# Polysketch attention with an ELU feed-forward: the key work of later batches in later steps, batch 1's key features through ScalarE, and one GpSimd rounding instead of four

## The chip, the cores and the metric

The kernel runs on one core of a Trainium2 chip. A core has five engines that run side by side, each with its own queue of instructions: TensorE (PE) for matrix products and its weight loads (PEld), VectorE (DVE), ScalarE (ACT), GpSimd (POOL) and SyncE (SP), which here only issues transfers. An engine takes its instructions in the order of the program and waits on semaphores for what other engines produce. The metric is the time of one execution on the device, in microseconds (us); lower is better.

## The reference

```
q, k, v: (4 batches, 4 heads, 1088 positions, 32) float32;  S1, S2: (8, 32)
phi(x)  = outer(S1 x, S2 x), flattened to 64 features per position
kv = sum over s of phi(k) v^T        (64 x 32 per batch and head)
z  = sum over s of phi(k)            (64 per batch and head)
x  = (phi(q) kv) / (phi(q) z + 1e-6)           -> (4352, 128) after the heads are joined
h  = x @ w_in                        (128 -> 2048)
g  = h if h > 0 else exp(h) - 1      (ELU)
out = g @ w_out                      (2048 -> 128)
```

S1, S2, w_in and w_out arrive as 64-bit floats. The kernel turns them into float32 itself ("rounding" below), by integer operations on the two halves of each number.

## The kernel before

**Tiling.** The 4352 rows are cut into 68 half tiles of 64 and these into 9 groups g of up to 512 rows (the last has 256). The hidden size 2048 is cut into 8 chunk pairs cp of 256. One **step** is one (g, cp). `mm1` makes h for both chunks of the pair (L661), `elu` is two ScalarE operations (L677, L679) and one VectorE operation (L685) per chunk, and `mm2` adds the pair into the output bank `o0` or `o1` (L698). In step n TensorE does `mm1` of step n and `mm2` of step n - 2; there are 72 steps, and groups 0 and 1 take turns in the first sixteen. The buffers of h are four, so `mm1` of step n can begin only when `elu` of step n - 2 is done. `fin1` transposes a finished group and issues its output transfers on SP.

**Rounding.** Eleven roundings i turn weights into float32 as they arrive: 0 to 5 are 256 columns wide, 6 to 10 are 512 wide (w_in and w_out of one chunk pair; rounding 6 serves pair 3, and so on to rounding 10 for pair 7). `RA(i)` is one VectorE mask (L99), `RB(i)` one ScalarE operation (L104), `RC(i)` three VectorE operations (L112, L113, L117) and a last one, `round_e`, which is either one VectorE operation (L125) or, with `pool`, two on GpSimd (L122, L123).

**Attention.** For each batch b the keys go through `transp` (VectorE transpose, L235), `KF_late` (key features, TensorE, L312) with `KF_late_out` (VectorE transposes, L322), `KO_late` (two outer products, VectorE, L282), `KA_late` (the sums kv and z, TensorE, L340 and L344) with `KC_late` (ScalarE copies), and `KZ_late` with `KZ_late_out` and `KZ3` (TensorE, VectorE, GpSimd), which leave kvp and SWp for the queries. Batch 0 has its own functions ahead of the steps (`KF`, `KF_out`, `KO`, `KA`, ...; L298 and L397 are its key features and sums). Queries: `transp` of q, then `queries(g5, g1)` on TensorE, which holds the last product of group g5 (`q5`, L627) and the first of group g1 (`q1`, L492); `q1_out` (VectorE, L502), `q2` (VectorE, features) and `q4` (VectorE transpose, L617) lie between the two products of a group. `x0_eps` opens the sums of group 0 with four products that put 1e-6 into them (L554), `q1_first` is group 0's first product (L530). `keep_warm` multiplies ones into an unused bank (L221).

**Order.** The program is a list written by hand. Work ahead of the steps stands in plain order; in the steps, `at(n, f, ...)` puts a call between `mm1` and `elu` of step n, and `late(n, f, ...)` puts it after `elu` and ahead of `mm2`. The order within each engine's queue is that of these calls. Small PSUM tiles share the tag `aux` with two banks. Transfers are issued on SP in one list; the key and query tiles of a batch have two buffers each, so a load waits for the transpose that frees its buffer.

Of the kernel before, what the change touches and what calls it, by code (L numbers as in the profile page):

```python
# [12 lines left out]
F32 = mybir.dt.float32  # L13
# [9 lines left out]
def _ap(ap: bass.AP, free):  # L23
    return dataclasses.replace(ap, ap=[list(ap.ap[0])] + [list(x) for x in free])
# [3 lines left out]
def kernel(  # L28
# [20 lines left out]
    nc = tc.nc  # L49
    B, H, S, D = q.shape  # L50
    R = S1.shape[0]
    P = 128
# [4 lines left out]
    NT = S // 64  # L57
    KT = (NT + 1) // 2
# [5 lines left out]
    work = ctx.enter_context(tc.tile_pool(name="wk", bufs=2))  # L64
    psum = ctx.enter_context(tc.tile_pool(name="psum", bufs=2, space=bass.MemoryType.PSUM))
# [6 lines left out]
    kT = [const.tile([FD, 2 * KT, 64], F32, name=f"kT{b}") for b in range(B)]  # L72
    qT = [const.tile([FD, NT, 64], F32, name=f"qT{b}") for b in range(B)]
# [145 lines left out]
    def keep_warm(n, cols=256):  # L219
        for i in range(n):  # L220
            nc.tensor.matmul(idle[:, :cols], some[:, :P], some[:, :cols], skip_group_check=True)  # L221
# [12 lines left out]
    def transp(dst, x, b, t0, t1):  # L234
        nc.vector.transpose(dst[b][:, t0:t1, :].rearrange("p t (a c) -> p c t a", c=2), hd[x, b][:, :, t0:t1, :])  # L235
# [11 lines left out]
    Sab = const.tile([FD, H, 2 * R], F32, name="Sab")  # L247
    SW = const.tile([FD, H, 3, R], F32, name="SW")
    SWp = const.tile([FD, B, 2, 4, R], F32, name="SWp")
    keep_warm(3)  # L250
    keep_warm(1, 160)
    sps = psum.tile([P, 512], F32, name="sps", tag="aux")
    nc.tensor.matmul(sps[:, :2 * R], Sx[:].rearrange("p h d -> p (h d)"), ident[:2 * R, :2 * R])
    make_SX()
# [10 lines left out]
    def make_SXh():  # L265
        nc.gpsimd.tensor_add(Sxp[:].rearrange("p x c r -> p c x r"), Sab[:, :2].rearrange("p c (x r) -> p c x r", x=2),
                             Sab[:, 2:].rearrange("p c (x r) -> p c x r", x=2))
        nc.gpsimd.tensor_add(pmask[:], bmask[:, :2], bmask[:, 2:])
        nc.vector.tensor_reduce(hmask[:], _ap(zmask[:], [[1, H], [H, 4]]), axis=AX, op=ADD)
        nc.gpsimd.tensor_mul(SXh[:].rearrange("p (h d) -> p h d", h=H), SX[:].rearrange("p (h d) -> p h d", h=H),  # L270
                             _ap(hmask[:], [[1, H], [0, D]]))

    def make_SWp():
        nc.gpsimd.memset(SWp[:, :, :, 3, :], 0.0)
        for b in range(B):
            nc.gpsimd.tensor_add(SWp[:, b, :, :2, :].rearrange("p c x r -> p c (x r)"), Sab[:, :2], Sab[:, 2:])


    def outer(dst, ab):

        a_, b_ = ab[:, :, 1, :], ab[:, :, 0, :]
        nc.vector.tensor_mul(dst, _ap(a_, list(a_.ap[1:]) + [[0, R]]), _ap(b_, [b_.ap[1], [0, R], b_.ap[2]]))  # L282
# [6 lines left out]
    kv_ps, feats, zms, wzs, abps = {}, {}, {}, {}, {}  # L289
# [11 lines left out]
        abps[b] = [where[i] for i in (0, 4, 8)]  # L301

    def KF_late(b):
# [25 lines left out]

    def KA_late(b):

        kv = kv_ps[b] = psum.tile([P, 512], F32, name="kvl", **(dict(tag="aux") if b == 1 else dict(tag="o1", bufs=1)))
        ab = feats.pop(b)
        kp = [feats.pop((b, half)) for half in range(2)]
        for i in range(KT):
            for h in range(H):
                nc.tensor.matmul(kv[32 * h:32 * h + 32, :R * R], vt[b][:, (h * KT + i) * D:(h * KT + i + 1) * D],  # L340
                                 kp[i // 5][:, i % 5, h].rearrange("p i j -> p (i j)"),
                                 start=(i == 0), stop=(i == KT - 1), skip_group_check=True, tile_position=(0, 32 * h))
            c = 32 * (i % 4)
            nc.tensor.matmul(kv[c:c + 32, R * R:R * R + H * R], ab[:, 0, i].rearrange("p h r -> p (h r)"),  # L344
                             ab[:, 1, i].rearrange("p h r -> p (h r)"),
                             start=False, stop=(i >= KT - 4), skip_group_check=True, tile_position=(0, c))
# [29 lines left out]
    def KO(b, gi):  # L376
        ab, rows = feats[b, gi]
        n = len(KG[gi])
        kp = work.tile([P, 4, H, R, R], F32, name="kp", tag="kp", bufs=3)
        outer(kp[:rows, :n].rearrange("p t h i j -> p (t h) i j"),  # L380
              ab[:rows, :n].rearrange("p t h x r -> p (t h) x r"))
        feats[b, gi] = kp, rows
# [43 lines left out]
    def KZ3(b):  # L426
        z = wzs.pop(b)
        nc.gpsimd.tensor_add(SWp[:, b, :, 2, :], z[:, :2], z[:, 2:])
# [6 lines left out]
    def KS(b):  # L435
        nc.gpsimd.memset(kvp[:, b], 0.0)
        for hp in range(2):
            for f in range(2):
                for e in range(2):
                    r = 64 * e + 32 * hp  # L440
                    nc.gpsimd.tensor_copy(kvp[r:r + 32, b, f, :, hp, :],
                                          kvz[b][64 * hp + 32 * f:64 * hp + 32 * f + 32, :, hp, :D])
# [10 lines left out]
    def half_tile(g, k):  # L453
        return divmod(8 * g + k, NT)
# [70 lines left out]
    def q1_first():  # L525
        p = psum.tile([P, 512], F32, name="abqp", tag="aux")
        for i in range(4):
            for u in range(2):
                b, t = half_tile(0, 2 * i + u)
                nc.tensor.matmul(p[64 * u:64 * u + 64, i * 64:i * 64 + 64], qT[b][:, t, :],  # L530
                                 Sab[:].rearrange("p h y -> p (h y)"),
                                 skip_group_check=True, tile_position=(0, 64 * u))
        x = work.tile([P, 4 * H, 2, R], F32, name="abq", tag="abq", bufs=1)
        nc.scalar.copy(x[:].rearrange("p m x r -> p (m x r)"), p[:, :4 * 64])
        abw[0] = x
# [14 lines left out]
    def x0_eps():  # L550
        xps = []
        for tt in range(2):
            p = psum.tile([P, 512], F32, name="x0ps", tag="h", bufs=4)
            nc.tensor.matmul(p[:, :8 * (D + 1)], some[:1, :P], eps[:].rearrange("p m d -> p (m d)"),  # L554
                             start=True, stop=False, skip_group_check=True)
            xps.append(p)
        return xps
# [43 lines left out]
    def q5_second():  # L601
        xp = [psum.tile([P, 512], F32, name="xps", tag="aux") for _ in range(2)]
        for h in range(H):
            for w in range(2):
                nc.tensor.matmul(xp[w][D * h:D * h + D, :256], kvS[64 * w:64 * w + 64, h, :],
                                 qpT[1][64 * w:64 * w + 64, h].rearrange("p m s -> p (m s)"),
                                 skip_group_check=True, tile_position=(64 * w, D * h))
        xg[1] = work.tile([P, 512], F32, name="xg", tag="xg", bufs=2)
        to = xg[1][:].rearrange("p (m w s) -> p w m s", w=2, s=P)
        for w, copy in enumerate((nc.scalar.copy, nc.vector.tensor_copy)):  # L610
            copy(to[:, w], xp[w][:, :256].rearrange("p (m s) -> p m s", s=P))
# [120 lines left out]
            eng.dma_start(rows[b, :, t:t + n, :], o[64 * u:64 * u + 64])  # L732


    x0 = x0_eps()
    transp(kT, "k", 0, 0, KT)
    transp(kT, "k", 0, KT, NT)
    KF(0)
# [1 line left out]
    transp(qT, "q", 0, 0, 8)  # L740
    KO(0, 0)
    q1_first()
    KO(0, 1)
    KO(0, 2)
    RA(0)
# [20 lines left out]
    round_w(round_c, 2)  # L766
    RA(3)
    q5_second()
    make_SWp()
    KZ3(0)  # L770
    KS(0)
    make_SXh()
    keep_warm(1)
    for c in range(2):
        elu_a(0, 1, c)
# [14 lines left out]
    def at(n, f, *a):  # L790
        extra.setdefault(n, []).append((f, *a))

    def late(n, f, *a):
        extra.setdefault((n, 1), []).append((f, *a))

    for n, i in ((2, 3), (3, 4), (4, 6), (5, 5), (6, 7), (8, 8), (10, 9), (12, 10)):
        if i > 3:
            at(n - 1, RA, i)
            late(n - 1, RB, i)
        at(n, RC, i, i > 6)  # L800


    for b, (n_t, n_f, n_o, n_a, n_z, n_q) in enumerate(
            ((3, 5, (6, 7), 8, 10, 9), (11, 12, (13, 14), 19, 20, 21), (17, 18, (20, 21), 22, 24, 25)), 1):
        at(n_t, transp, kT, "k", b, 0, NT)
        at(n_f, KF_late, b)
        late(n_f, KF_late_out, b)
        for half in range(2):
            at(n_o[half], KO_late, b, half)
        at(n_a, KA_late, b)  # L810
        late(n_a, KC_late, b)
        at(n_z, KZ_late, b)
        late(n_z, KZ_late_out, b)
        late(n_z, KZ3, b)
        at(n_q, transp, qT, "q", b, 0, NT)
    at(13, queries, None, 2)
    for g in range(2, NQ):
        n = NP * (g - 1)
# [56 lines left out]
```

## Time and profile before

| | |
|---|---|
| median of 4 runs | 284.16 us (282.75 to 284.42) |
| profiled execution | 283.3 us, span 281.5 us |
| mean granted TensorE clock | 0.993 |
| busy in the span | TensorE 272.7 us, ScalarE 179.8, VectorE 178.8, GpSimd 20.6 |
| step of 512 rows on TensorE | 1.72 us for `mm1` and 1.72 us for `mm2` |
| first product of the first step in the loop (step 2) | at 23.98 us |

The span runs from the first to the last instruction of one profiled execution; the time of that execution has 1.8 us around it. Durations in the text are of that execution. A matrix product of float32 shows as two records, each with a weight load. A record's duration holds the time that it takes to pass through the engine, so the time from one start to the next is what counts for a queue. A row of the waits reads: engine and line that waited, what released it, total time, number of times, longest.

### The profile page before, as it was taken

To read this page: it belongs to the slowest core of one execution; us is meant where nothing else is said; L and a number is where in the kernel's file an instruction comes from. 1 tells how busy PE (TensorE), PEld (TensorE's weight loads), DVE (VectorE), ACT (ScalarE), POOL (GpSimd) and SP (SyncE) were. 2 spreads that over 40 slices of the span, in tenths; PEclk is the share of its full clock that TensorE was granted. 3 is DMA by queue.
4 is the path that set the end of the run, shared out by engine and by line. 5 is a ranking of instruction groups with operands and counts; after the bars stand their busy time and mean duration, and the time that the engine had idled before them with its cause. 6 is when DMAs were issued, how large, how long until landed. Compare 5 with 4: busy or idle time off the path is not lost.

```text
span 281.5 us, 3800 instructions
## 1 busy us (share of the span) xinstructions
PE 272.7 (97%) x1348; PEld 137.3 (49%) x1348; DVE 178.8 (64%) x319; ACT 179.8 (64%) x337; POOL 20.6 (7%) x55
## 2 busy tenths in 40 slices
PE   8999998999989999999999999999999999999994
PEld 6874333543344545444444454444444444444694
DVE  5988999899947695467634663466444734573442
ACT  2468876676546464666766665666566666667682
POOL 4160004333000000000000000000000000000000
PEclk9799999999999999999999999999999999999999
DMA  6995790110002200002000100020002000100020
GB/s 180 336 326 159 209 250 14 29 53 0 0 2 37 40 1 2 0 4 34 3 0 10 28 2 0 0 34 5 0 2 37 0 1 0 24 16 0 5 33 19
DMA packets 25474, 13.35 MB, mean 47 GB/s; under 512 B 18416, under 2 KB 23664, under 8 KB 25456
## 3 DMA queue, kind: packets, MB, share of 16 engines
q1 hardware_dynamic: 24944, 12.66, 18.0%
q10 hardware_dynamic: 512, 0.46, 0.5%
q8 instruction: 10, 0.16, 0.2%
q14 instruction: 8, 0.07, 0.1%
HBM read 10.88 MB, written 2.23 MB: 47 GB/s over the span
## 4 chain that ended last, share of the span: by engine, by line
PE 86%; DVE 6%; DMA 2%; issue 1%; POOL 1%; ACT 1%; SPq 1%; POOLq 0%; DVEq 0%
PE h L661 37%; PE o L698 36%; PE ol L721 3%; PE qps L627 2%; DMA v<-in_v_dram 2%; DVE gg L685 2%; PE kvl L340 1%; PE kv L397 1%; PE qps L492 1%; POOL raw L122 1%; PE x0ps L569 1%; DVE raw L117 1%; PE h L668 1%; DVE W L112 1%; PE kfps L312 0%
## 5 line engine op out<-in xcount | busy, mean ns | idle before, releaser
L685 DVE SCALAR_TENSOR_TENSOR gg<-e,h 128x512 f32<-128x512 f32 (+1 forms) x144 | 93.1, 656 | 89.5 <-ACT e L679 89.3
L661 PE MATMUL h<-xg,W 128*128 128x512 f32 (+1 forms) x284 | 126.9, 569 | 1.5 <-POOL W L123 1.1
L677 ACT ACTIVATE e<-h 128x512 f32<-128x512 f32 (+1 forms) x144 | 81.3, 564 | 72.5 <-PE h L661 72.3
L698 PE MATMUL o<-gg,W 128*128 128x512 f32 x256 | 121.6, 597 | 0.0
L679 ACT ACTIVATE e<-e 128x512 f32<-128x512 f32 (+1 forms) x144 | 87.3, 606 | 4.6
L661 PEld LDWEIGHTS h<-xg,W 128*128 128x128 f32 x284 | 53.3, 190 | 63.8 <-issue 51.9
L698 PEld LDWEIGHTS o<-gg,W 128*128 128x128 f32 x256 | 47.3, 190 | 56.3 <-issue 55.3
L104 ACT ACTIVATE W<-W,ebias 128x256 uint32<-128x256 uint32 (+1 forms) x11 | 6.6, 600 | 6.1 <-DVE W L99 6.1
L520 DVE TENSOR_TENSOR qp<-an,abw 128x1024 f32<-128x1024 f32 (+1 forms) x9 | 9.3, 1046 | 0.3
L627 PE MATMUL qps<-qpT,kvp 64*64 64x256 f32 (+3 forms) x136 | 7.4, 339 | 1.5 <-DVE qpT L617 1.5
L721 PEld LDWEIGHTS ol<-W,gg 128*128 128x128 f32 x64 | 8.1, 192 | 0.3
L282 DVE TENSOR_TENSOR kpl<-abk 128x1280 f32<-128x1280 f32 (+1 forms) x6 | 8.1, 1351 | 0.0
L617 DVE STREAM_TRANSPOSE qpT<-qp 128x1024 f32<-128x1024 f32 (+1 forms) x7 | 8.1, 1161 | 0.0
L721 PE MATMUL ol<-W,gg 128*128 128x128 f32 x64 | 8.1, 275 | 0.0
L627 PEld LDWEIGHTS qps<-qpT,kvp 64*64 64x64 f32 x136 | 4.7, 132 | 6.6 <-issue 3.1
L122 POOL TENSOR_TENSOR raw<-raw,tiny 128x512 f32<-128x512 f32 x4 | 5.3, 1337 | 32.3 <-DVE raw L117 32.3
L502 DVE STREAM_TRANSPOSE abw<-qps 128x256 f32<-128x256 f32 (+1 forms) x14 | 5.2, 407 | 2.0 <-ACT xg L639 2.0
L117 DVE SCALAR_TENSOR_TENSOR raw<-raw 128x256 f32<-128x256 uint32 (+1 forms) x11 | 6.0, 549 | 0.3
L112 DVE SCALAR_TENSOR_TENSOR W<-raw,W 128x256 uint32<-128x256 uint32 (+1 forms) x11 | 5.9, 539 | 0.0
L705 DVE STREAM_TRANSPOSE ob<-o 128x512 f32<-128x512 f32 x8 | 5.7, 710 | 0.1
L639 ACT COPY xg<-qps 128x256 f32<-128x256 f32 x12 | 3.9, 374 | 2.8 <-PE qps L492 2.8
L235 DVE STREAM_TRANSPOSE qT<-hd_q 128x1088 f32<-128x1088 f32 (+2 forms) x5 | 5.4, 1079 | 0.3 <-DMA hd_q<-in_q_dram 0.3
(118 smaller groups left out, 132.9 us busy)
## 6 DMA issues: line engine op xcount, KB each, us to landing
raw<-in_moe_w_in_dram SPq DMA_DIRECT2D x8, 256.0 KB, 6.4
raw<-in_moe_w_out_dram SPq DMA_DIRECT2D x8, 256.0 KB, 6.2
hd_k<-in_k_dram SPq DMA_DIRECT2D x3, 544.0 KB, 8.2
hd_q<-in_q_dram SPq DMA_DIRECT2D x3, 544.0 KB, 3.3
out_dram<-ob SPq DMA_DIRECT2D x40, 32.0 KB, 1.7
v<-in_v_dram SPq DMA_DIRECT2D x4, 288.0 KB, 8.4
v<-in_v_dram SPq DMA_DIRECT2D x4, 256.0 KB, 8.4
hd_k<-in_k_dram SPq DMA_DIRECT2D x1, 288.0 KB, 3.5
```

The costliest lines, as they stand in the source:

```text
L112: nc.vector.scalar_tensor_tensor(d, hi, 0x80000000, d, op0=AND, op1=OR)
L117: nc.vector.scalar_tensor_tensor(lo.bitcast(F32), lo, 2.0 ** -32, raw[:, :, 1], op0=MUL, op1=ADD)
L122: nc.gpsimd.tensor_mul(mant, mant, _ap(tiny[:], [[0, dst.shape[1]]]))
L282: nc.vector.tensor_mul(dst, _ap(a_, list(a_.ap[1:]) + [[0, R]]), _ap(b_, [b_.ap[1], [0, R], b_.ap[2]]))
L520: nc.vector.tensor_mul(qp[g][:, h], _ap(a_, list(a_.ap[1:]) + [[0, R]]), _ap(b_, [b_.ap[1], [0, R], b_.ap[2]]))
L627: nc.tensor.matmul(ps[e][64 * g2:64 * g2 + 64, 64 * k:64 * (k + m)], kvp[r, b, f, g2].rearrange("p c d -> p (c d)"), qpT[g][r, n * g2 + 2 ...
L661: nc.tensor.matmul(hs[g, cp][c][:, :n], W[:, cp, c * P:c * P + P], xg[g][:, :n])
L677: nc.scalar.activation(e, hs[g, cp][c][:, :n], RELU, scale=-1.0)
L679: nc.scalar.activation(e, e, EXP, scale=-1.0)
L685: nc.vector.scalar_tensor_tensor(gs[g, cp][:, c, :n], es[g, cp][:, c, :n], -1.0, hs[g, cp][c][:, :n], op0=ADD, op1=MAX)
L698: nc.tensor.matmul(ops[g][:, :n], W[:, cp, (2 + c) * P:(3 + c) * P], gg[:, c, :n], start=(first and c == 0), stop=(last and c == 1))
L721: nc.tensor.matmul(ops[g][i][:], gg[:, c, i * P:i * P + P], W[:, cp, (2 + c) * P:(3 + c) * P], start=(first and c == 0), stop=(last and c ...
```

## The change

Ahead of the steps, the warm-up products shrink from 160 to 64 columns, a warm-up of 96 columns stands where `x0_eps` stood, and `x0_eps` follows `q1_first`. `make_SWp`, `KZ3(0)`, `KS(0)` and `make_SXh` (GpSimd work, with one VectorE reduction, L269) move from ahead of the steps to the ends of steps 2, 3 and 4. Of the roundings only number 7 keeps its last operation on GpSimd; 8, 9 and 10 get it on VectorE. Batch 1's key features are made by a new function, `KF_second`, in the manner of batch 0's: 18 products that need no transposes behind them, and two ScalarE copies. Its outer products, sums and z work come one or two steps later, and its query transpose earlier, at the end of step 6. The key work of batches 2 and 3 moves to later steps, batch 3's sums to bank `o0`, and the query transposes are written out one by one.

```diff
-    keep_warm(1, 160)
+    keep_warm(1, 64)
...
+    def KF_second(b):
+        ps = [psum.tile([P, 512], F32, name="abp", tag="aux") for _ in range(2)]
+        for i in range(KT):
+            for u in range(2):
+                nc.tensor.matmul(ps[i // 5][64 * u:64 * u + 64, 64 * (i % 5):64 * (i % 5) + 64],
+                                 kT[b][:, u * KT + i, :], Sab[:].rearrange("p h y -> p (h y)"),
+                                 skip_group_check=True, tile_position=(0, 64 * u))
+        ab = feats[b] = work.tile([P, 2, KT, H, R], F32, name="abk", tag="abk", bufs=2)
+        for j in range(2):
+            t = slice(0, 5) if j == 0 else slice(5, KT)
+            n = t.stop - t.start
+            nc.scalar.copy(ab[:, :, t].rearrange("p x t h r -> p x (t h) r"),
+                           ps[j][:, :64 * n].rearrange("p (m x r) -> p x m r", x=2, r=R))
...
-        kv = kv_ps[b] = psum.tile([P, 512], F32, name="kvl", **(dict(tag="aux") if b == 1 else dict(tag="o1", bufs=1)))
+        kv = kv_ps[b] = psum.tile([P, 512], F32, name="kvl", **(dict(tag="aux") if b == 1 else dict(tag=f"o{3 - b}", bufs=1)))
...
-    x0 = x0_eps()
+    keep_warm(1, 96)
...
     q1_first()
+    x0 = x0_eps()
     KO(0, 1)
...
     q5_second()
-    make_SWp()
-    KZ3(0)
-    KS(0)
-    make_SXh()
     keep_warm(1)
...
-        at(n, RC, i, i > 6)
+        at(n, RC, i, i == 7)
+
+    late(2, make_SWp)
+    late(3, KZ3, 0)
+    late(3, KS, 0)
+    late(4, make_SXh)
...
-    for b, (n_t, n_f, n_o, n_a, n_z, n_q) in enumerate(
-            ((3, 5, (6, 7), 8, 10, 9), (11, 12, (13, 14), 19, 20, 21), (17, 18, (20, 21), 22, 24, 25)), 1):
+    for b, (n_t, n_f, n_o, n_a, n_z) in enumerate(
+            ((3, 5, (7, 9), 10, 11), (15, 16, (17, 18), 19, 20), (18, 20, (24, 25), 27, 29)), 1):
         at(n_t, transp, kT, "k", b, 0, NT)
-        at(n_f, KF_late, b)
-        late(n_f, KF_late_out, b)
+        if b == 1:
+            at(n_f, KF_second, b)
+        else:
+            at(n_f, KF_late, b)
+            late(n_f, KF_late_out, b)
...
-        at(n_q, transp, qT, "q", b, 0, NT)
+    late(6, transp, qT, "q", 1, 0, NT)
+    at(21, transp, qT, "q", 2, 0, NT)
+    at(30, transp, qT, "q", 3, 0, NT)
```

## The prediction

> **What bounds the kernel now.** I read the page's busy times first, then the waits of TensorE alone, then the windows of the steps in which those waits lie, and last the timelines of VectorE and GpSimd there.
>
> ```profile
> PE 272.7 (97%) x1348; PEld 137.3 (49%) x1348; DVE 178.8 (64%) x319; ACT 179.8 (64%) x337; POOL 20.6 (7%) x55
> ...
> PE qps L627 <- DVE qpT L617: 1.5, 1, 1.5
> PE idle L221 <- DVE warm L144: 1.2, 1, 1.2
> PE h L661 <- POOL W L123: 1.1, 1, 1.1
> PE kv L397 <- DMA v<-in_v_dram: 0.6, 1, 0.6
> PE h L661 <- DVE W L125: 0.3, 1, 0.3
> ```
>
> TensorE is busy 97% of the span, so nothing but less TensorE work or fewer of these few waits can help. The start and end of the program aside, there are three waits in the step loop (1.5, 1.1 and 0.3 us) and one for v before it. From about 82 us the chain of work runs through TensorE without a hole: 1.72 us for a step's first product, 1.72 for the second, 3.43 a step.
>
> ```profile
> 34.93:39.21 4.28, 4.28 (x26) 1.62 (x25) 4.11 (x10) 2.32 (x6) 0.00 (x0) 1.00 1.05 286
> 39.21:42.64 3.43, 3.43 (x9) 1.52 (x8) 3.40 (x8) 3.05 (x6) 0.00 (x0) 1.00 0.92 184
> 42.64:47.39 4.75, 3.60 (x10) 1.33 (x8) 4.71 (x6) 2.70 (x5) 3.51 (x2) 1.00 0.04 12
> ...
> 43.58 1.49 DVE L282 TENSOR_TENSOR kpl<-abk 128x1280 f32<-128x1280 f32 x1
> 44.98 1.28 DVE L685 SCALAR_TENSOR_TENSOR gg<-e,h 128x512 f32<-128x512 f32 x2
> 46.18 1.44 DVE L99 TENSOR_SCALAR W<-raw 128x512 uint32<-128x512 uint32 x1
> ...
> 43.74 2.22 POOL L122 TENSOR_TENSOR raw<-raw,tiny 128x512 f32<-128x512 f32 x1 [19.23 <-DVE raw L117]
> 46.04 1.29 POOL L123 TENSOR_TENSOR W<-raw,W 128x512 f32<-128x512 f32 x1
> ```
>
> The first three rows are steps 5, 6 and 7 (columns: stretch, its length, then busy time of TensorE, its weight loads, VectorE, ScalarE, GpSimd; clock; DMA share). VectorE is full in all of them. In step 7 TensorE stands still until GpSimd has finished rounding chunk pair 4 (rounding 7) at 47.33; step 8 starts at 47.39, 1.31 us after the previous product's 44.36 + 1.72. GpSimd's first half took 2.22 us, against 1.04 in its three later instances.
>
> ```profile
> 74.77 1.22 DVE L282 TENSOR_TENSOR kpl<-abk 128x1024 f32<-128x1024 f32 x1
> 75.90 1.28 DVE L685 SCALAR_TENSOR_TENSOR gg<-e,h 128x512 f32<-128x512 f32 x2
> 77.10 1.24 DVE L617 STREAM_TRANSPOSE qpT<-qp 128x1024 f32<-128x1024 f32 x1
> ...
> 78.48 1.16 PE L627 MATMUL qps<-qpT,kvp 64*64 64x64 f32 x24 [1.50 <-DVE qpT L617]
> ```
>
> This is the other wait: an outer product of batch 2's keys stands between group 2's features and their transpose, which step 15's query products await.
>
> **Step loop, VectorE.** Costs are start-to-start times from the timelines: activation pair 1.19 us, rounding 2.54 on 512 columns and 1.59 on 256, final rounding operation alone 0.60, mask of the next rounding 0.34 or 0.20, transpose of a batch 1.23, outer products 1.40 and 1.13, key-feature transposes (L322) 0.77.
> Steps 2 to 7 before: 2.98 + 4.35 + 3.93 + 3.89 + 4.5 + 3.7 = 23.4 us, against TensorE's 6 x 3.43 + 0.84 for key features = 21.4: VectorE is behind. After: step 5 loses 0.77, step 6 swaps the 1.40 product for the 1.23 query transpose, step 7 swaps the 1.13 product for the 1.40 one and loses the 1.0 us stretch of L99; a 0.1 us reduction (L269) comes into step 4. Sum 21.6 against about 21.9. VectorE just keeps up.
> Steps 8 to 12 after: 3.73 + 2.66 + 3.73 + 1.96 + 3.73 = 15.8, with three times 0.60 that GpSimd did before, against TensorE's 5 x 3.43 + 1.64 (L340, L344) + 0.40 (L355, L357) = 19.2. These roundings are free; without that cover they would cost 1.8.
>
> **Rounding 7.** It stays on GpSimd, but what follows it on VectorE is now the activation pair and the query transpose. I follow the queues: ScalarE's two new copies end near 38.7, step 5's activations near 41.7, VectorE's part of rounding 7 at 43.6, GpSimd ends near 46.1; step 8's product is due at 46.3. The margin is 0.2. Here a rule matters. The row's mean over four instances is 1337 ns for L122, which would give 43.6 + 1.34 + 1.34 = 46.3, just in time. The Trainium skill, page "SBUF — State Buffer", section "SBUF: two separate sides", says that a VectorE operation with two SBUF inputs and a GpSimd operation that reads SBUF exclude each other for the whole instruction, the earlier one winning. By it the 2.22 was 1.2 of waiting behind the outer product begun at 43.58, and with no such operation there now it is 1.04 + 1.30 = 46.0. I take the rule; if a stretch of 1.2 comes back, 1.0 of gain goes. Gain here: 1.31 (range 0.3 to 1.31).
>
> **Group 2.** Steps 13 and 14 lose both outer products of batch 2. From step 13's start T: its activations end at T + 4.11, the query transposes take 0.8, features 2.43, next pair 1.19, then the transpose of 1.24: the products can start at about T + 9.9. Before, with 1.13 more, it was 67.43 + 11.05. TensorE gets there at T + 9.5. So 1.13 goes and about 0.4 stays.
>
> **Batch 1's key features.** Eight products in two passes (16 records, 0.65 us) become 36. The nearest row is L298, the same shape: its last 32 weight loads run from 6.55 in 1.01 us, 31 ns apart; 36 x 31 = 1.12. Extra: 0.47 us on TensorE, fully on the path. Bounds: 0.3 to 1.1 (the slower 50 ns of half clock). ScalarE's two copies (320 and 256 columns; rows of 256 take 374 ns, of 384 479 ns) are about 0.8 and wait for those products; queued behind them are step 5's activations and rounding 7's RELU. The activations come some 1.4 us later, but TensorE needs their buffers only in step 7, over 1.5 us later still.
>
> **Later batches.** Their transposes, outer products, sums and queue order move to steps 15 to 30. VectorE's fullest stretch there, steps 17 to 20, is about 3.3 + 3.6 + 3.6 + 3.6 = 14.1 us against 4 x 3.43 + 1.64 + 0.40 + 0.84 = 16.6 of TensorE, and group 3's transpose is ready some 3 us ahead of step 22. TensorE's own work is only moved. Cost zero; without that cover up to 1.2 at one place. PSUM banks o1 and o0 are free two steps before the sums take them. On SP's queue the load of batch 3's queries, held until 54.53 by batch 1's query transpose, goes some 9 us earlier into an idle DMA stretch; nothing waits behind it until the first output at 86.66.
>
> **GpSimd preparation (SWp, kvp, SXh).** It is moved in program order only: nothing on GpSimd's queue stands ahead of it that waits longer, and even before it ran early:
>
> ```profile
> 14.69 0.15 POOL L274 MEMSET SWp<- 128x64 f32 x1
> 14.90 0.87 POOL L276 TENSOR_TENSOR SWp<-Sab 128x32 f32<-128x32 f32 x4
> ```
>
> Its line came after work done at 23.4. I count zero (between -0.1 and +0.1); the reduction L269 leaves 0.1 less before rounding 4: -0.1.
>
> **Opening.** The warm-up is 96 columns in two passes shorter, some 0.3 us at the opening's rate (160 columns: 0.27 each), so the first products come near 4.25 instead of 4.57 and the key features about 0.25 earlier; queries wait for their load until 6.75 anyway, so L530 begins near 7.5. Then the four sum-opening products, which ran at 5.12 in 0.22 each and cost nothing (transposes were awaited), stand before the kv sums, which v holds until 9.30.
>
> ```profile
> 4.55:7.96 3.41, 3.28 (x51) 2.58 (x52) 2.50 (x5) 0.82 (x3) 0.35 (x3) 0.99 1.10 269
> 7.96:11.37 3.41, 2.78 (x56) 2.62 (x52) 3.41 (x5) 1.17 (x4) 0.00 (x0) 0.51 1.06 336
> ```
>
> The granted clock is 0.51 in just that stretch. By the wait of 0.63 alone, 0.9 us of products fit with 0.1 or so to spare for the earlier start: change 0. By the Trainium skill, page "TensorE: Matmul & The Clock Gate", section "Part 1: The HAM clock gate", the clock is halved for windows of 3.4 us after one not busy enough; the stretch above has that length. Then the four take 1.78 from 8.0 and the sums start at 9.8. They run 50 ns apart at half clock and 35 at full (weight loads of L397): 31 cold and 41 warm end 0.35 later than 41 and 31. I take +0.4, range -0.2 to +0.9. TensorE has no slack from there to step 2, so it counts whole.
>
> **Sum.** -1.31 - 1.13 + 0.47 - 0.1 + 0.4 = -1.7 us (the terms are rounded). The profiled execution took 283.3 (span 281.5 and 1.8 around it), giving 281.6. It lies 0.9 under the median of four runs, 284.16; less 1.7 that is 282.4, my number.
>
> **Rivals.** (1) The opening is free, the clock being up when the four products come or the gap swallowing them: -2.2, 281.9 or a little lower. For it: 0.63 of idle time; against: the 0.51. (2) Rounding 7 is late again, by a lock or by ScalarE's copies: -0.7, 283.5. The margin of 0.2 speaks for it, the absence of a two-input operation against. (3) Slower: the shorter warm-up leaves the first window too empty and the clock stays at half beyond 4.55. Until 11.37 this costs 0.5 over my forecast (features and L530 at 50 ns end near 8.8, the four at 10.6), until 14.78 about 1.6, until 18.2 another 1.7. It decides against the change only in the last case: -2.1 + 3.7 = +1.6, 285.8. TensorE is full from 1.18 to about 4.1 of those 3.4 us even so, which speaks against. (4) The change doesn't do what it says: the GpSimd part, as shown, doesn't move; that alone is worth nothing either way.
>
> **Chances.** Forecast 0.50, (1) 0.13, (2) 0.17, (3) with its milder ends and other slow openings 0.20, about 0.13 of it over half a percent slower. Half a percent (1.4 us) is about what a measurement of this kernel can tell from no change, and my forecast lies only 0.3 beyond it. Faster 0.60, same 0.27, slower 0.13. The range 281.0 to 284.6 takes in (1) and (2), the opening's bounds and the mild ends of (3).
>
> **What would show it.** Right: no wait of L661 on GpSimd; the wait of the query products on the transpose 0.4 to 0.6; GpSimd's only rounding about 1.04 + 1.3; 36 records for batch 1's key features in about 1.1 us; SWp still near 15 us; kv sums starting near 9.8. Wrong: a new wait of TensorE between steps 5 and 12, a clock under 1 after 11.4, or a first step product clearly later than 24.4.

## The result and the profile after

The changed kernel is faster: a median of 281.85 us (280.69 to 285.27, 37 runs) against 283.88 us (282.42 to 284.87, 56 runs); the ratio is 0.9937, with a 95% interval of 0.992 to 0.9953. That is 1.8 us by the ratio and 2.0 by the medians; 1.7 was forecast. The ratios, here and below, leave out executions more than 1.5% above the fastest of their kernel (4 of these 37); the mean over all executions fell by 1.4 us. The profiled execution took 281.85 us, its span 279.9 us.

The page's busy times and the waits of TensorE alone, after. L676 is `mm1` (L661 before), L642 the last query product (L627 before):

```profile
PE 274.1 (98%) x1370; PEld 139.5 (50%) x1370; DVE 178.3 (64%) x320; ACT 180.2 (64%) x339; POOL 12.1 (4%) x49
...
PE idle L221 <- DVE warm L144: 1.2, 1, 1.2
PE qps L642 <- DVE qpT L632: 0.4, 1, 0.4
PE h L676 <- DVE W L125: 0.3, 1, 0.3
```

The wait on GpSimd is gone and that on the transpose is down from 1.5 to 0.4 us. In all, TensorE is busy 1.4 us longer (272.7 before) while the span is 1.6 us shorter.

The windows of steps 5, 6 and 7, and the timelines of GpSimd and VectorE around rounding 7:

```profile
35.14:39.97 4.83, 4.83 (x46) 2.57 (x45) 4.66 (x12) 2.64 (x7) 0.51 (x1) 1.00 1.06 290
39.97:43.40 3.43, 3.43 (x10) 1.52 (x8) 3.29 (x8) 3.33 (x7) 0.00 (x0) 1.00 0.60 135
43.40:46.83 3.43, 3.43 (x9) 1.52 (x8) 3.43 (x6) 2.76 (x6) 2.35 (x2) 1.00 0.01 2
...
43.56 1.04 POOL L122 TENSOR_TENSOR raw<-raw,tiny 128x512 f32<-128x512 f32 x1 [4.66 <-DVE raw L117]
44.68 1.30 POOL L123 TENSOR_TENSOR W<-raw,W 128x512 f32<-128x512 f32 x1
...
43.39 1.28 DVE L700 SCALAR_TENSOR_TENSOR gg<-e,h 128x512 f32<-128x512 f32 x2
44.59 1.31 DVE L235 STREAM_TRANSPOSE qT<-hd_q 128x1088 f32<-128x1088 f32 x1
45.81 0.45 DVE L99 TENSOR_SCALAR W<-raw 128x512 uint32<-128x512 uint32 x1
```

Step 7 is down from 4.75 to 3.43 us, the length of a step that waits for nothing; step 5 is up from 4.28 to 4.83. GpSimd's first operation takes 1.04 us where it took 2.22. It ends the rounding at 45.98, 0.85 ahead of step 8's product at 46.83.

VectorE ahead of group 2's transpose, and the query products of step 15 that wait for it:

```profile
72.12 1.23 DVE L535 TENSOR_TENSOR qp<-an,abw 128x1024 f32<-128x1024 f32 x1
73.26 1.28 DVE L700 SCALAR_TENSOR_TENSOR gg<-e,h 128x512 f32<-128x512 f32 x2
74.46 1.24 DVE L632 STREAM_TRANSPOSE qpT<-qp 128x1024 f32<-128x1024 f32 x1
...
75.84 1.16 PE L642 MATMUL qps<-qpT,kvp 64*64 64x64 f32 x24 [0.36 <-DVE qpT L632]
```

The outer product (L282) that stood between the features and the activation pair is gone from there.

The **step loop** can be measured apart from the opening: from step 2's first product to the first product of the last step (the last step of all has no other TensorE work but `mm2_last` behind it). That is 23.98 to 274.16 before, 250.18 us, and 24.19 to 272.56 after, 248.37 us: 1.81 us less. Step by step, in TensorE's start times:

| | before | after | difference |
|---|---|---|---|
| step 5: batch 1's key features | 4.28 | 4.83 | +0.55 |
| step 7: wait for rounding 7 | 4.75 | 3.43 | -1.32 |
| step 15: query products of group 2 | 6.73 | 5.59 | -1.14 |
| steps 8 to 29: key work moved, net | | | +0.10 |
| sum | | | -1.81 |

The rest of the 1.6 us in the span is the opening, 0.21 us longer in this execution.

### The profile page after: what moved, and what is told of

Read it like the earlier page. It is cut to its first block, busy times and chain, and to the rows that moved or that the text cites. A ratio compares the mean times of both kernels' runs of the same rounds, so it can differ in the third digit from the quotient of the medians.

```text
span 279.9 us, 3833 instructions
## 1 busy us (share of the span) xinstructions
PE 274.1 (98%) x1370; PEld 139.5 (50%) x1370; DVE 178.3 (64%) x320; ACT 180.2 (64%) x339; POOL 12.1 (4%) x49
## 4 chain that ended last, share of the span: by engine, by line
PE 89%; DVE 5%; ACT 3%; issue 1%
PE h L676 37%; PE o L713 36%; PE ol L736 3%; PE qps L642 2%; DVE gg L700 2%; PE kvl L355 1%; PE idle L221 1%; ACT e L694 1%; ACT e L692 1%; PE qps L507 1%; PE kv L412 1%; PE abp L298 1%; PE x0ps L584 1%; PE h L683 1%; DVE raw L117 1%
## 5 line engine op out<-in xcount | busy, mean ns | idle before, releaser
L676 PE MATMUL h<-xg,W 128*128 128x512 f32 (+1 forms) x284 | 126.8, 569 | 0.4 <-DVE W L125 0.3
L676 PEld LDWEIGHTS h<-xg,W 128*128 128x128 f32 x284 | 53.5, 190 | 62.2 <-issue 51.4
L282 DVE TENSOR_TENSOR kpl<-abk 128x1280 f32<-128x1280 f32 (+1 forms) x6 | 8.0, 1339 | 0.0
L642 PE MATMUL qps<-qpT,kvp 64*64 64x256 f32 (+3 forms) x136 | 7.4, 339 | 0.4 <-DVE qpT L632 0.4
L642 PEld LDWEIGHTS qps<-qpT,kvp 64*64 64x64 f32 x136 | 4.7, 132 | 6.1 <-PE h L676 5.7
L221 PE MATMUL idle<-some 128*128 128x256 f32 (+2 forms) x12 | 4.7, 543 | 1.2 <-DVE warm L144 1.2
L125 DVE SCALAR_TENSOR_TENSOR W<-raw,W 128x256 f32<-128x256 f32 (+1 forms) x10 | 5.3, 531 | 0.3
L235 DVE STREAM_TRANSPOSE kT<-hd_k 128x1088 f32<-128x1088 f32 (+2 forms) x5 | 5.3, 1071 | 0.0
```

The source lines that it names most:

```text
L642: nc.tensor.matmul(ps[e][64 * g2:64 * g2 + 64, 64 * k:64 * (k + m)], kvp[r, b, f, g2].rearrange("p c d -> p (c d)"), qpT[g][r, n * g2 + 2 ...
L676: nc.tensor.matmul(hs[g, cp][c][:, :n], W[:, cp, c * P:c * P + P], xg[g][:, :n])
```

## The experiments

The loop's length comes out the same to 0.02 us in the changed kernel and its variants with the same loop, and to 0.06 in the two kernels with the loop of before, so it carries the verdicts of 0.1 to 1 us. Medians and ratios also hold the opening, which varies by 2 us and more from one execution to the next.

### The opening alone and the loop alone

`e1_opening_back` is the changed kernel with the old opening:

```diff
-    keep_warm(1, 64)
+    keep_warm(1, 160)
...
-    keep_warm(1, 96)
+    x0 = x0_eps()
...
     q1_first()
-    x0 = x0_eps()
```

> The changed kernel with the opening of before (160 columns of warm-up, the sum-opening products ahead of the key features). Theory (the gain lies in the step loop, the opening costs some 0.2 to 0.4 us): ratio to before about 0.9925 to 0.994, the loop from step 2 to the end as in the changed kernel (255.7 us from step 2's first product to the span's end), step 2 starting near 24.0 at the same clock pattern. Rival (the opening brings a part of the gain, through the clock): ratio 0.996 or more, and step 2 later than 24.2.

Measured: loop 248.36 us, step 2 at 23.78, median 281.61 us (16 runs), ratio 0.9943 (0.9925 to 0.9962), a little above the range that the theory gave.

`e2_opening_only` is the kernel before with the reverse of this edit.

> The kernel before with the new opening alone. Theory: 0 to +0.4 us, ratio 1.000 to 1.0015; the loop from step 2 to the end stays 257.5 us. Rival (the opening brings a part of the gain): ratio 0.998 or less, step 2 earlier than 23.98.

Measured: loop 250.12 us, median 283.6 us (22 runs), ratio 0.9995 (0.9975 to 1.0016). The profiled execution of this one has a late opening, with step 2 at 27.54, so it says nothing of the usual start.

The whole gain is in the loop; the new opening is worth nothing that the ratios can tell, in either kernel. In the means over all executions it costs 0.4 us in both (282.24 us for the changed kernel against 281.83 for `e1`, 284.12 for `e2` against 283.72 for the kernel before), with a standard error of 0.3 us in either; some executions then open late, and these are counted below.

### Batch 1's key features

`e3_key1_late`:

```diff
-        if b == 1:
-            at(n_f, KF_second, b)
-        else:
-            at(n_f, KF_late, b)
-            late(n_f, KF_late_out, b)
+        at(n_f, KF_late, b)
+        late(n_f, KF_late_out, b)
```

> The changed kernel with batch 1's key features made as before (8 products, two VectorE transposes at the end of step 5), all else as changed. Theory of the queues: TensorE saves 0.55 us in step 5, but VectorE's 0.77 put rounding 7 later and step 8's product waits 0.3 to 0.6 us for it, so within 0.2 us of the changed kernel. Rival (the ScalarE copies are what frees VectorE): the wait for rounding 7 comes back whole, 1.2 us, and the kernel is 0.7 us slower than the changed one. Other rival (VectorE had slack enough): no wait, 0.5 us faster than the changed one.

Measured: loop 248.20 us, 0.17 less than the changed kernel; step 5 is back at 4.28, step 7 is 3.72 and step 8 pays another 0.1. Median 282.01 us (22 runs), ratio 0.9947 (0.9928 to 0.9966). So the new function saves a wait of 0.39 us and costs 0.55 of TensorE's time. The queue theory held, and neither rival did: the old form would have been as good.

### The lock between VectorE and GpSimd

`e4_product_at_6` lets the first outer product follow rounding 7 again:

```diff
-            ((3, 5, (7, 9), 10, 11), ...
+            ((3, 5, (6, 9), 10, 11), ...
...
-    late(6, transp, qT, "q", 1, 0, NT)
+    at(7, transp, qT, "q", 1, 0, NT)
```

> The changed kernel with batch 1's first outer product back in step 6, right behind VectorE's part of rounding 7, and the query transpose in its place in step 7. VectorE's sum of work over steps 6 and 7 is the same. Theory of the lock: GpSimd's first operation of rounding 7 takes 2.2 us again instead of 1.04, step 8's product waits about 1.0 us for it, the kernel is 1.0 us slower than the changed one. Rival (VectorE's amount of work up to step 7 decides): GpSimd's operation near 1.04, no wait, no change against the changed kernel.

GpSimd and VectorE there:

```profile
43.79 2.22 POOL L122 TENSOR_TENSOR raw<-raw,tiny 128x512 f32<-128x512 f32 x1 [4.67 <-DVE raw L117]
46.09 1.29 POOL L123 TENSOR_TENSOR W<-raw,W 128x512 f32<-128x512 f32 x1
...
43.63 1.48 DVE L282 TENSOR_TENSOR kpl<-abk 128x1280 f32<-128x1280 f32 x1
45.03 1.28 DVE L700 SCALAR_TENSOR_TENSOR gg<-e,h 128x512 f32<-128x512 f32 x2
46.23 1.44 DVE L99 TENSOR_SCALAR W<-raw 128x512 uint32<-128x512 uint32 x1
```

The 2.22 us and the 1.44 us of the kernel before are back, to the hundredth, with VectorE's work in steps 6 and 7 the same in sum. So it is which operations meet, not how much work there is. This is the case of the Trainium skill's page "SBUF — State Buffer", section "SBUF: two separate sides": the product began 0.16 ahead of GpSimd's operation, and that one ends 0.90 after the product, where it takes 1.04 alone. Beside the activation pair and the query transpose, in the changed kernel, GpSimd's two operations were not stretched. That the two SBUF inputs are what matters is the page's word; the runs show only these pairs of operations. L99's 1.44 us (0.45 in the changed kernel) is a stretch too, behind GpSimd's second operation; but L99 reads one tile only, so the rule in the prediction's words does not cover it, and why it was held is not shown.

The price was only half of what I expected: loop 248.84 us, +0.47, because the margin ahead of step 8 was larger than I had worked out. Median 282.7 us, ratio 0.9979 (0.9956 to 1.0002). That is 0.85 us above the changed kernel's median, of which the loop explains 0.47; the rest lies outside the loop, in an opening whose code is the same.

### The other roundings and GpSimd's preparation

`e5_gpsimd_back`:

```diff
     q5_second()
+    make_SWp()
+    KZ3(0)
+    KS(0)
+    make_SXh()
     keep_warm(1)
...
-        at(n, RC, i, i == 7)
-
-    late(2, make_SWp)
-    late(3, KZ3, 0)
-    late(3, KS, 0)
-    late(4, make_SXh)
+        at(n, RC, i, i > 6)
```

> The changed kernel with the GpSimd part as before: roundings 7 to 10 end on GpSimd, and SWp, kvp and SXh are prepared ahead of the steps in program order. Theory (both were worth nothing): the loop, from step 2's first product to the end of TensorE's work, within 0.15 us of the changed kernel's 248.37; GpSimd's SWp work near 15 us in either. Rival (GpSimd's roundings were a part of the loss): a new wait of a step product on GpSimd of 0.3 us or more at steps 10, 12 or 14.

Measured: loop 248.37 us, the same to 0.01 as the changed kernel; median 281.75 us (19 runs), ratio 0.9927 (0.9908 to 0.9945). GpSimd's preparation in this kernel, and then in the changed one, where it stands at the ends of steps 2 and 3 in the program:

```profile
14.59 0.15 POOL L274 MEMSET SWp<- 128x64 f32 x1
14.80 0.88 POOL L276 TENSOR_TENSOR SWp<-Sab 128x32 f32<-128x32 f32 x4
```

```profile
14.85 0.15 POOL L274 MEMSET SWp<- 128x64 f32 x1
15.06 0.88 POOL L276 TENSOR_TENSOR SWp<-Sab 128x32 f32<-128x32 f32 x4
```

SWp and kvp run at the same point of the opening (GpSimd's zm, which precedes them, came at 13.22 and at 13.50). Only SXh moved, from 23.94 to 38.39: it waits for the reduction L269, which stands later in VectorE's queue now. And the lock went the other way once in this kernel, at rounding 8:

```profile
51.60 1.48 POOL L123 TENSOR_TENSOR W<-raw,W 128x512 f32<-128x512 f32 x1
...
51.84 2.32 DVE L282 TENSOR_TENSOR kpl<-abk 128x1024 f32<-128x1024 f32 x1
```

GpSimd was first, VectorE's outer product took 2.32 us for 1.22, and nobody waited for it: VectorE had that much room there.

### Group 2's transpose

`e6_batch2_early` puts batch 2's keys back:

```diff
-            ... (15, 16, (17, 18), 19, 20), ...
+            ... (11, 12, (13, 14), 19, 20), ...
```

> The changed kernel with batch 2's key features back in step 12 and its outer products back in steps 13 and 14. Theory: the wait of the query products on group 2's transpose goes from 0.36 to 1.5 us, all else stays, loop 248.37 + 1.13 = 249.5. Rival (the wait comes from rounding 10 or from ScalarE, not from the outer product): wait below 0.8 us.

Measured: loop 249.50 us, wait 1.49 us. Median 283.22 us (20 runs), ratio 0.998 (0.9959 to 1.0002). The waits of TensorE in this kernel:

```profile
PE qps L642 <- DVE qpT L632: 1.5, 1, 1.5
PE idle L221 <- DVE warm L144: 1.2, 1, 1.2
```

In the timeline an outer product stands between group 2's features and the activation pair again (it begins at 76.07, the pair at 77.21, 1.14 us later), and the loop is 1.13 us longer. The edit moves the rest of batch 2's key work back too, but the trace shows none of it in that queue between the features and the transpose. This one move is worth 1.13 of the loop's 1.81 us.

### The two halves of the new opening

`e7_long_warmup`:

```diff
-    keep_warm(1, 64)
+    keep_warm(1, 160)
```

> The changed kernel with the warm-up of 160 columns kept; the sum-opening products stay behind the first query products. The loop is the changed one's. It tells which half of the new opening causes executions over 283.5 us (9 of 37 of the changed kernel, none of 16 with the old opening). Theory A (the shorter warm-up lets the clock open a window later): none over 283.5. Theory B (the 1 us of dense products taken from between 5 and 6 us does): they stay, about a quarter.

Measured: median 281.99 us, ratio 0.9931 (0.9909 to 0.9953); 2 of 13 executions over 283.5 us.

`e8_sums_early`:

```diff
-    keep_warm(1, 96)
+    x0 = x0_eps()
...
     q1_first()
-    x0 = x0_eps()
```

> The changed kernel with the sum-opening products back ahead of the key features and the warm-up kept short (64 columns, without the 96). The loop is the changed one's. Theory A (the shorter warm-up lets the clock open a window later): about a quarter of the executions over 283.5 us. Theory B (the products taken from between 5 and 6 us do): none over 283.5.

Measured: median 282.1 us, ratio 0.9944 (0.9927 to 0.9961); none of 22 over 283.5 us.

Both counts are of all executions. With the sums opened early (`e1`, `e8`) none of 38 executions are over 283.5 us; with the sums opened late it is 9 of 37 (the changed kernel), 3 of 19 (`e5`), 5 of 22 (`e3`) and 2 of 13 (`e7`). Theory B fits all of them, though 2 of 13 alone would say little. The other kernels agree, if the limit is moved by the difference of their loops: 5 of 22 in `e2`, 9 of 22 in `e4` and 5 of 20 in `e6`, all with the sums opened late, and none of 17 in the two versions of the next section or of 56 of the kernel before, which open them early.

The profiled execution of `e7` is one of the late ones, and TensorE's timeline shows the price:

```profile
6.39 2.36 PE L298 MATMUL abp<-Sab,kT 128*64 128x64 f32 x34
8.54 1.07 PE L545 MATMUL abqp<-Sab,qT 128*64 128x64 f32 x16
9.54 2.12 PE L569 MATMUL x0ps<-eps,some 1*128 1x264 f32 x4
11.59 4.31 PE L412 MATMUL kv<-v,kp 128*64 128x64 f32 x72
```

The four products take 2.12 us for 1.17 in the profiled changed kernel, the sums 4.31 us for 2.46, and step 2 begins at 27.66 instead of 24.19. The granted clock reads 1.00 in that stretch, but only because the trace holds no entry of the clock before its first change. In `e7` that first entry, a change to full, comes at 17.35 us; in the profiled changed kernel at 9.38, during the first of the four products. The durations change at these points: in the changed kernel the first of the four starts 342 ns ahead of the second, and the next follow 223 and 222 ns apart, and in `e7` the products of L562 (128 columns) run 213 ns apart up to 17.36, against 109 in the changed kernel. `e6`'s profiled execution is late in another way, which the rows do show. Its PEclk row, and then that of `e7`, a slice being 7.1 us:

```profile
PEclk9599999999999999999999999999999999999999
PEclk9999999999999999999999999999999999999999
```

In `e6` the clock is full from 4.21 us, 0.50 from 7.63 to 14.45, and full again; its sums take 4.07 us. So a late opening is a longer time at half clock, and a row or a mean of 1.00 does not rule one out. Why the clock opens later without the four products in their old place is not shown; the runs give the counts alone.

### A version that takes only what pays

`e9_vector_only` has the old opening and the edit of `e3`, and besides

```diff
-        at(n, RC, i, i == 7)
+        at(n, RC, i, False)
...
-    late(6, transp, qT, "q", 1, 0, NT)
+    at(9, transp, qT, "q", 1, 0, NT)
...
-    at(13, queries, None, 2)
+    at(12, queries, None, 2)
...
-        n1, n2, n4, n5 = (13, 13, 14, 15) if g == 2 else ...
+        n1, n2, n4, n5 = (12, 12, 14, 15) if g == 2 else ...
```

> A version meant to be faster than both: the changed kernel with the opening of before, batch 1's key features made as before (no extra TensorE work), rounding 7 wholly on VectorE, batch 1's query transpose in step 9, and group 2's first query products and features in step 12 instead of 13. By following the queues: the wait for rounding 7 does not come back although VectorE transposes the key features again, the wait on group 2's transpose is gone, TensorE saves 0.55 in step 5: loop 248.37 - 0.55 - 0.36 = about 247.5 (range 247.4 to 247.9). Rival (rounding 7 needs GpSimd): a new wait of 0.3 us or more in steps 6 to 10, loop 248 or more.

`e10_vector_fill` adds `keep_warm(1, 128)` behind `q1_first()`.

> The same with a filling product of 128 columns (two passes) behind group 0's first query products, in the time that the wait for v leaves. Loop as in the version without it. Theory (the clock is held down by too little dense work between 4.5 and 8 us): the step loop begins 0.1 to 0.5 us earlier in the median. Rival (the filling is too late or too little): no change within 0.2 us, or 0.1 later where it delays the sums.

Measured: loops 247.65 and 247.63 us, 0.72 under the changed kernel and 2.5 under the one before; medians 281.38 (7 runs) and 281.44 us (10 runs), ratios 0.9919 (0.9889 to 0.9948) and 0.9909 (0.9881 to 0.9937). None of these executions opened late. TensorE's waits in `e9`:

```profile
PE h L676 <- DVE W L125: 0.3, 1, 0.3
PE xps L620 <- ACT qpT L614: 0.2, 1, 0.2
PE qps L642 <- DVE qpT L632: 0.2, 1, 0.2
```

No rounding on GpSimd is needed at all: VectorE ends rounding 7 at 45.68 us in `e9`, 1.54 ahead of step 8's product at 47.22. The query transpose stands behind that rounding in the queue either way, so its move is not what makes it early. The same may hold for the kernel before: VectorE's part of rounding 7 ended at 43.66 there, and its last operation takes 0.6 us, so by an estimate from these rows it would have ended near 44.3, ahead of 46.1, when step 8 could have begun. This was not run. Of the 0.72 us, 0.55 are step 5's and 0.18 step 15's; the wait on group 2's transpose went down from 0.36 to 0.2, not to nothing as expected. The loop is shown to be shorter; that the whole kernel is faster than the changed one is not, since the intervals overlap. The filling product did not move the median by 0.2 us, so the rival of that run stands.

## Why the prediction was right

**Rounding 7: -1.31 forecast, -1.32 measured.** The mechanism was the one told, and `e4` shows it. GpSimd took 1.04 and 1.30 us, as the forecast by the page's rule had it, and not the row's mean of 1337 ns. But the margin that I gave it, 0.2 us, was 0.85, so the mean would have forecast the same gain; it is `e4` that tells the two apart. Against step 2, GpSimd ended 0.33 us earlier than my list of the queues said, and step 8's product came 0.32 later. Of that, 0.08 is step 5's growth beyond the forecast, and the rest a slip: step 5's start of 34.93 and steps of 4.75, 3.43 and 3.43 make 46.5, not 46.3. Rival (2), which drew its chance from that margin, was weaker than its 17%.

**Group 2: -1.13 forecast, -1.14 measured,** with 0.4 us of wait left as told; `e6` gives the reverse.

**Batch 1's key features: +0.47 forecast, +0.55 measured.** The 36 records took 1.2 us from the first start to the next product, 0.08 more than 36 times 31 ns. What the forecast did not say is that the term buys little: `e3` shows that without it the loop is 0.17 shorter.

**Later batches: 0 forecast, +0.10 measured.** No wait arose. But batch 3's sums, which shared step 22 with the query products, stand alone in step 27 (step 22 is 1.34 shorter, step 27 1.54 longer), while batch 1's cost 0.1 less in step 10 than in step 8, where they followed a wait.

**GpSimd's preparation: 0 forecast; loop unchanged in `e5`.** The gain of 0.1 us from moving the reduction L269 did not come. The time it left ahead of step 2 went into a wait of VectorE for ScalarE's exponential (0.30 us, none there before), and step 4's product starts 0.47 us late in both kernels.

**Opening: +0.4 forecast, +0.21 in the profiled pair, nothing in the ratio of `e2`.** This term is not confirmed. The size in the profiled pair is within the range given, but that is luck, since what happened there is not what was told. The forecast kept the half clock where it had been, from 7.96 to 11.37 us. In the profiled changed kernel it lay earlier, up to 9.38: the key features ran at half the rate (2.29 us of the chain for 34 records), and of the four sum-opening products only the first was still slow. The kv sums started at 10.42, not 9.8, and then took 2.46 us instead of 3.37. The 3.4 us that the prediction took for a window is the length of the half clock in the kernel before (3.41 us), but the 3.41 us ahead of it were 96% busy by the profile (3.28 us), so busy time did not tell when the clock would be halved. What I called rival (3), a clock that stays at half well beyond 4.55 us, occurs in a mild form in this execution and in a costly one in about a quarter of the changed kernel's. By the counts it goes with the move of the sum-opening products, not, as I wrote, with the shorter warm-up; the median is spared.

**The sum: -1.7 forecast, -1.8 by the ratio.** Its three large terms came within 0.1 us each. That the whole did too is partly luck: the loop was to gain 2.07 us and gained 1.81, and the opening was to cost 0.4 and cost 0.21 in the profiled pair. Rival (1), a free opening, is not ruled out by the times: its 281.9 us is nearer to the measured median of 281.85 than my 282.4, and by the medians the change is worth 2.0. Part of that is the base: the 56 executions put the kernel before at 283.88 us, 0.28 under the four that I counted from. Three more sums do not come out as written: VectorE's work in steps 2 to 7 adds to 21.8 us by its own terms, not 21.6, so its room against 21.9 was smaller than told; rival (1) adds to -2.07, not -2.2; and 284.16 less 1.7 is 282.5. None of them changes the forecast's direction.

## What to carry to other kernels

Where the engine of the chain is busy 97% of the span, list its few waits and follow each back through the releasing engine's queue. Here the length of one wait and the duration of one outer product gave the two large terms to 0.02 us. The margin behind the first, added up over several queues, was off by 0.65 us, so a small margin found that way decides little. When an operation on GpSimd sits on the path, look at what VectorE starts just ahead of it: an outer product with two SBUF inputs stretched it from 1.04 to 2.22 us here. Then ask whether GpSimd is needed; `e9` did without it. A call moved to a later place in the program moved nothing on GpSimd where its inputs were ready and its queue was empty (SWp), and moved the work by 14 us where an input came from an operation of VectorE that was moved too (SXh); look in the trace where it ran.

## What was not expected of the hardware

- The step loop repeats to 0.02 us between the changed kernel and its variants with the same loop (248.37, 248.36, 248.37, 248.36, 248.37) and to 0.06 between the kernel before and `e2` (250.18, 250.12), while the opening, ahead of 24 us, differs by over 3 us between executions of nearly the same code (step 2 at 23.78, 24.19, 27.66).
- Four products with a single row (4 records of 264 columns, 1 to 2 us) ahead of the key features go with the absence of late openings: none of 38 executions with them there (`e1`, `e8`), 19 of 91 in the changed kernel and its variants `e3`, `e5` and `e7` without them.
- The granted clock in the rows can read 1.00 at half rate: in `e7` the trace's first entry of the clock comes at 17.35 us, and the products ahead of it ran 213 ns apart for 109.
- The lock cost either engine about 1.1 us: GpSimd's 1.04 became 2.22, and VectorE's 1.22 became 2.32 when GpSimd was first. In each case this is 0.14 us less than what was left of the other's operation (1.32 and 1.24 us).
